# Attention visits of four scores instead of three where a visit holds an AV, from the fourth stage on

## The chip, the cores and the metric

The kernel runs on one core of a Trainium2 chip. The metric is the device time of one execution in microseconds (us). The engines that matter are TensorE (PE, matrix multiplies into PSUM), ScalarE (ACT), VectorE (DVE), GpSimd (POOL) and the queue of SyncE (SP), which issues most transfers. Each engine works through its own instructions in a fixed order, and waits on semaphores where it needs the result of another.

## The reference

Cosine attention over q, k, v of shape 8 x 12 x 448 x 64 (batch, heads, positions, width), then a feed-forward pair of matrices:

```
q_n = q / (norm(q) + 1e-6);  k_n = k / (norm(k) + 1e-6)
scores = q_n @ k_n.T / tau
attn = softmax(scores)
x = (attn @ v), heads side by side      # 3584 x 768
h = x @ w_in                            # 3584 x 2048
out = (h * cos(h)) @ w_out              # 3584 x 768
```

## The kernel before

**Units of work.** Two pairs of heads of one batch item make a quad; a batch item has three quads, the whole problem 24 (0 to 23). A quad is worked in seven steps. One step is a `scores` (L592 to L609): four 64 x 64 matmuls with 448 columns on PE (L601) into a pair of PSUM banks, then one exponential on ACT over 128 x 896 elements (L608), which empties that pair into a tile E. When all seven E of a quad exist, a `gather` (L628 to L649) does the quad's AV: 28 matmuls of E with V (L637) into a pair of banks, and a copy on DVE to AVs (L644). The row sums of two quads come from one `sums` (L711 to L755): 28 matmuls of E with a selecting matrix (L724) into one bank, Ln and Exp on ACT (L733, L734) for the reciprocal, a transfer by SP to a scratch tensor in memory (L737), four transfers by SP that read it back spread over the partitions (tile R, L743), and a product on POOL for each quad (L748), which writes xT, the input of the feed-forward part. Which quads share a round of sums is the list `ROUNDS` (L863); the last is quads 22 and 23.

**The feed-forward part.** m1 (L768 to L802) is, for one batch item, 96 matmuls of W1 with xT (L774) in eight pairs of banks; h * cos(h) of each pair runs through ACT (L792), DVE (L793), ACT (Sin, L795) and DVE (L798). Exponentials with Ln, and Sin, lie in two activation tables; a change of table is a load on ACT (L412). m2 (L823 to L857) multiplies the result with W2: sixteen matmuls of 384 columns (L833) for each half of an output tile of 128 rows, then a copy on DVE (L851) and, for each whole tile, transfers to the output by SP (L857).

**Stages.** The first three quads run in a head whose order is written out by hand. Then a loop over c = 0 to 7 (L1093 to L1194) makes eight stages. Stage c does m1 of batch item c, and after that m2 of the same item, into which the scores and AVs of later quads are woven: `STEPS` (L861) gives 35, 28, 21, 21, 21, 21, 0 and 0 steps, so quads 15 to 17 are scored in stage c = 3 (the fourth), 18 to 20 in c = 4, 21 to 23 in c = 5, and none in the last two.

**Visits.** Scores, AV and sums use tiles of 64 x 64 or 128 x 32 of the PE array, m1 and m2 the whole array. So the steps of a stage are cut into groups, called visits, by `visits_of` (L875 to L890). It takes `PER` = 3 steps for each. If a quad was finished in an earlier visit (`owed`), its AV is put into the visit behind two scores (`AT` = 2). A round of sums becomes due when its last quad is finished.

**Banks of a visit.** Scores and AVs take the three pairs of banks that m1 has left, in turn (`slot`, L892). So a score may start only when the exponential of the score (or the AV copy) three takings earlier has emptied its pair.

**Between visits** stands m2 work, cut to size by `fill(n)` (L1141): n matmuls of the list `items` of the stage. 24 come ahead of the first visit, 8 behind it (L1183, with nothing due), and behind every other visit a share of what is left: visits without an AV weigh 3, those with one 2 (`WE`), and `MOST` = 14 is the limit (L1182, L1183). `fill` also places a due round of sums, where the m2 tile that runs is between its fifth and its thirteenth matmul (L1138). In the last two stages, without visits, three banks serve m2, and a round that is still due goes in after ten matmuls (L1148 to L1150).

**Order on the engines.** The class `Planner` records each operation with a cost and what it reads and writes, and then orders ACT, DVE, POOL and SP by planned times. PE keeps the order of the program. Three short runs of operations are moved forward or back by their number (`LEADS`, L107 to L111); the run from operation 1169 lies in m1 of stage c = 4.

Of the kernel before, what the change touches and what calls it, by code (L numbers as in the profile page):

```python
# [304 lines left out]
def bass_cosine_attention__then__act_gcu_kernel(  # L305
# [16 lines left out]
    NNB = FF // 128  # L322
# [227 lines left out]
    def norm_b(qd, eng="pool", after=()):  # L550
        for _ in inverse(qd, 0, 2, after=after):
            pass
        for w in range(2):
            last = scale(qd, w, eng)
        return last
# [306 lines left out]
    MOST, WE = 14, (3, 2)  # L862
    ROUNDS = [[FIRST, FIRST + 1], [FIRST + 2]] + [[i, i + 1] for i in range(FIRST + 3, NQ, 2)]  # L863
    E1, E2, SLO, SHI = NNB - 6, NNB - 4, 4, 12
    PER, AT, EC = 3, 2, 0
    due = []
# [5 lines left out]

    owed, carried, events = [], [], [0]

    def visits_of(quads):  # L875

        steps = [divmod(g, NJ) for g in quads]
        out, late = [], []
        while steps:
            what, steps = steps[:PER], steps[PER:]  # L880
            mine, late = late, []
            for p, (qd, j) in enumerate(what):
                if j == NJ - 1:
                    (late if p or not steps else mine).extend(x for x in ROUNDS if x[-1] == qd)
            ended = [qd for qd, j in what if j == NJ - 1]
            if owed:
                what.insert(AT, (owed.pop(0), None))
            owed.extend(ended)
            out.append((what, mine))
        return out, late  # L890
# [5 lines left out]
    def visit(what):  # L896
        for qd, j in what:
            if j == 0:
                begin(qd)
            if j is None:  # L900
                gather(qd, slot())
            else:
                scores(NJ * qd + j, slot())
        for qd, j in what:
            if j == 0 and FIRST < qd < NQ - 3:
                norm_a(qd + 3, [o for o in P.ops if o.eng == "dve"][-1:])
            if j == 3 and FIRST < qd < NQ - 4:
                load_qk(qd + 4)
            if (qd, j) == (FIRST + 1, 3):
                bs = slot()  # L910
                for w in range(2):
                    transpose(FIRST + 2, w, bs + w)
            if j == NJ - 1 and qd + 2 < NQ:
                if qd > FIRST:
                    turn(qd + 2)
# [176 lines left out]
    done = NJ * FIRST  # L1092
    for c in range(B):  # L1093
# [47 lines left out]
        def fill(n):  # L1141
            while due and due[0][0] <= at[0] + n and len(banks) == 2 and at[0] + n < len(items) and not any(map(can_sum, range(at[0], at[0] + n))):
                n += 1
            n = min(n, len(items) - at[0])
            split = due and not can_sum(at[0])
            while n > 0:
                t, h, f0 = items[at[0]]
                if len(banks) == 3:  # L1148
                    if due and at[0] >= E1:
                        sums(due.pop(0)[1], free + 1)  # L1150
                elif due and can_sum(at[0]) and not (split and callable(due[0][1]) < can_sum(at[0] + n)):
                    what = due.pop(0)[1]
                    more = (what if callable(what) else lambda bk: sums(what, bk))(13 - cur[0])
                    due.extend((at[0] + 3 + 3 * i, x) for i, x in enumerate(more or ()))
                f1 = f0
                while n > 0 and f1 < NNB and items[at[0]:at[0] + 1] == [(t, h, f1)]:
                    at[0] += 1
                    f1 += 1
                    n -= 1
                    if due and can_sum(at[0]) and (n == 0 or not can_sum(at[0] + n)):  # L1160
                        break
                if (t, h) not in bank_of:
                    cur[0] = banks[(banks.index(cur[0]) + 1) % len(banks)] if cur[0] in banks else banks[0]
                    bank_of[t, h] = cur[0]
                m2(t, h, f0, f1, bank_of[t, h])
            if due and split and can_sum(at[0]) and not callable(due[0][1]) and len(banks) == 2:
                due.extend((at[0] + 3 + 3 * i, x) for i, x in enumerate(sums(due.pop(0)[1], 13 - cur[0]) or ()))

        new = done + STEPS[c]
        visits, over = visits_of(range(done, new))  # L1170
        if visits:
            visits[0][1].extend(carried)
            carried.clear()
            fill(FILLS[c][0] if c in FILLS else 2 * E2)
        for i, (what, mine) in enumerate(visits):
            if c == 0 and i == 1:
                spared.extend([x([o for o in P.ops if o.eng == "dve"][-1:]) for x in adds])
                norm_b(FIRST + 2, after=[o for o in P.ops if o.chain][-1:])
            visit(what)
            due.extend((0, r) for r in mine)  # L1180
            left = len(items) - at[0]
            weigh = [WE[sum(j is None for _, j in x)] for x, _ in visits[i:]]  # L1182
            even = 2 * (NNB - E2) + 3 * len(due) if i == 0 else min(MOST, -(-left * weigh[0] // sum(weigh)))  # L1183
            fill(FILLS[c][i + 1] if c in FILLS else even)
        if visits and new == NJ * NQ:
            gather(owed.pop(0), slot())
# [3 lines left out]
        done = new  # L1190
# [40 lines left out]
```

## Time and profile before

| what | value |
|---|---|
| median of three runs | 419.74 us (418.62 to 419.95) |
| the profiled execution | 419.27 us |
| its span in the trace | 417.5 us |
| PE busy | 408.4 us |
| ACT busy | 305.1 us |
| granted TensorE clock | 1.00 |

The span is the time from the first to the last recorded instruction; the execution has 1.77 us around it. Starts in the trace are counted from the start of the span. In the views, a line such as L601 is the line of the kernel that recorded the operation. A row of the timeline gives the start, the time, the engine, the line, what is written from what, and how many instructions are merged in it; a bracket behind it gives the idle time ahead of them and what ended it. A row of the chain of waits gives the start, the time and the engine whose work the end of the program hangs on there.

### The profile page before, as it was taken

What the parts mean: (1) busy time and instruction counts of PE and PEld (TensorE: products, weight loads), DVE (VectorE), ACT (ScalarE), POOL (GpSimd) and SP (SyncE); (2) the same over time, 40 slices, a digit from 0 to 9 for tenths busy, and PEclk for the clock granted to TensorE, in tenths of its full rate; (3) what the DMA queues carried; (4) which work ended last, traced back from release to release, by engine and by line L of the source; (5) the groups of instructions that cost most, each with busy time, mean ns of one, the idle gap of its engine ahead of it and who ended that gap; (6) DMA issues with size and microseconds to landing.
All of it is one profiled execution on the core that took longest, in us unless ns stands there. A gap on an engine that the chain in (4) does not pass through costs nothing.

```text
span 417.5 us, 8622 instructions
## 1 busy us (share of the span) xinstructions
PE 408.4 (98%) x3629; PEld 216.7 (52%) x3629; DVE 266.0 (64%) x359; ACT 305.1 (73%) x422; POOL 209.3 (50%) x145
## 2 busy tenths in 40 slices
PE   7999998999999999999999999999999999999997
PEld 7454544445554545555555555554554555555565
DVE  5887986638857549654985429845872328736931
ACT  6999899978888768897787747987797657605700
POOL 3668948996289862588419762477403113000000
PEclk9999999999999999999999999999999999999999
DMA  8999997999349994199617993099303523021023
GB/s 270 260 252 216 270 198 150 209 294 262 90 89 238 248 269 107 42 224 249 154 16 179 167 338 98 10 220 174 91 2 82 129 67 101 1 77 38 2 69 82
DMA packets 67223, 62.97 MB, mean 151 GB/s; under 512 B 36384, under 2 KB 59632, under 8 KB 67184
## 3 DMA queue, kind: packets, MB, share of 16 engines
q1 hardware_dynamic: 54816, 50.57, 47.9%
q0 software_dynamic: 12288, 11.80, 17.8%
q8 instruction: 28, 0.46, 0.4%
q14 instruction: 11, 0.09, 0.1%
q10 hardware_dynamic: 80, 0.05, 0.0%
HBM read 54.79 MB, written 11.15 MB: 158 GB/s over the span
## 4 chain that ended last, share of the span: by engine, by line
PE 80%; ACT 7%; DVE 5%; POOL 3%; DMA 2%; issue 1%; SPq 1%; POOLq 0%
PE PS L833 32%; PE PS L774 31%; PE PS L601 7%; PE PS L637 6%; ACT E L608 4%; PE PS L724 3%; DVE gT L798 2%; DVE ar L793 1%; DMA Qf<-in_q_dram 1%; DMA Kf<-in_k_dram 1%; POOL Qn L542 1%; POOL sqq L491 1%; PE PS L810 1%; ACT ar L676 1%; DVE AVs L644 1%
## 5 line engine op out<-in xcount | busy, mean ns | idle before, releaser
L608 ACT ACTIVATE E<-PS 128x896 bf16<-128x896 f32 x168 | 143.5, 921 | 20.5 <-PE PS L601 19.2
L833 PE MATMUL PS<-W,gT 128*128 128x384 bf16 x880 | 153.4, 327 | 0.0
L774 PE MATMUL PS<-xT,W 128*128 128x448 bf16 x768 | 147.7, 353 | 0.4 <-POOL xT L748 0.3
L833 PEld LDWEIGHTS PS<-W,gT 128*128 128x128 bf16 x880 | 81.9, 98 | 69.1 <-issue 16.0
L774 PEld LDWEIGHTS PS<-xT,W 128*128 128x128 bf16 x768 | 74.3, 98 | 71.3 <-issue 1.5
L792 ACT ACTIVATE ar<-PS 128x896 int32<-128x896 f32 (+1 forms) x72 | 58.8, 827 | 47.0 <-PE PS L774 46.9
L793 DVE SCALAR_TENSOR_TENSOR ar<-ar,PS 128x896 f32<-128x896 int32 (+1 forms) x72 | 69.2, 980 | 34.0 <-ACT ar L792 34.0
L748 POOL TENSOR_TENSOR xT<-AVs,R 128x896 bf16<-128x896 f32 x20 | 41.7, 2089 | 65.9 <-DMA R<-rscr 65.9
L798 DVE TENSOR_TENSOR gT<-PS,ar 128x896 bf16<-128x896 f32 (+1 forms) x72 | 69.3, 983 | 1.9 <-ACT ar L795 1.6
L795 ACT ACTIVATE ar<-ar 128x896 f32<-128x896 f32 (+1 forms) x72 | 60.6, 861 | 8.5 <-DVE ar L793 7.8
L851 DVE COPY osb<-PS 128x384 f32<-128x384 f32 x54 | 30.0, 556 | 53.6 <-PE PS L833 52.9
L542 POOL TENSOR_TENSOR Qn<-Qf,rr 128x896 bf16<-128x896 f32 x21 | 35.4, 1685 | 44.5 <-DVE rr L530 44.4
L601 PE MATMUL PS<-qT,kT 64*64 64x448 bf16 x672 | 48.9, 358 | 2.8 <-DVE kT L575 1.4
L644 DVE COPY AVs<-PS 128x896 f32<-128x896 f32 x21 | 22.8, 1088 | 35.3 <-PE PS L637 35.3
L491 POOL TENSOR_TENSOR sqq<-Qf 128x896 bf16<-128x896 f32 x21 | 35.2, 1677 | 7.3 <-DVE n L495 5.5
L491 POOL TENSOR_TENSOR sqk<-Kf 128x896 bf16<-128x896 f32 x21 | 35.2, 1676 | 6.2 <-DVE Kn L542 6.1
L542 POOL TENSOR_TENSOR Kn<-Kf,rr 128x896 bf16<-128x896 f32 (+1 forms) x22 | 36.7, 1666 | 0.0
L637 PE MATMUL PS<-E,Vb 64*64 64x448 bf16 x588 | 31.5, 350 | 0.4 <-ACT E L608 0.4
L601 PEld LDWEIGHTS PS<-qT,kT 64*64 64x64 bf16 x672 | 15.2, 105 | 27.3 <-issue 10.9
L451 POOL DMA_DIRECT2D Vb<-in_v_dram x24 | 18.1, 755 | 16.7 <-PE PS L601 10.3
L495 DVE TENSOR_REDUCE n<-sqk 128x14 f32<-128x896 bf16 (+2 forms) x24 | 24.9, 1039 | 1.8 <-POOL sqk L491 1.2
L495 DVE TENSOR_REDUCE n<-sqq 128x14 f32<-128x896 bf16 (+2 forms) x24 | 24.8, 1037 | 0.8 <-POOL sqq L491 0.6
(68 smaller groups left out, 200.5 us busy)
## 6 DMA issues: line engine op xcount, KB each, us to landing
Qf<-in_q_dram SPq DMA_DIRECT2D x24, 448.0 KB, 5.1
out_dram<-osb SPq DMA_DIRECT2D x54, 192.0 KB, 2.8
Kf<-in_k_dram SPq DMA_DIRECT2D x23, 448.0 KB, 6.1
R<-rscr SPq DMA_DIRECT2D x40, 224.0 KB, 4.4
Vb<-in_v_dram POOLq DMA_DIRECT2D x24, 224.0 KB, 5.9
W<-in_moe_w_in_dram POOLq DMA_DIRECT2D x4, 768.0 KB, 10.7
W<-in_moe_w_out_dram POOLq DMA_DIRECT2D x4, 768.0 KB, 12.5
Kf<-in_k_dram SPq DMA_DIRECT2D x1, 320.0 KB, 4.6
```

The source lines that it names most:

```text
L491: op(eng, (1.64 if eng == "pool" else 1.05) * n, lambda e: e.tensor_tensor(dst, src, src, ALU.mult), r=cut(nm + "f", s, part), w=at, after ...
L495: return op("dve", 0.05 + 0.94 * n, lambda e: e.tensor_reduce(out=n2[u].ap()[:, H * w:H * w + H] if part == ALL[0] else jr(n2[u], w, part) ...
L542: lambda e: e.tensor_tensor(n[u].ap()[:, j0:j1].rearrange("p j r d -> p r j d"), f[s].ap()[:, :, j0:j1], rb, ALU.mult),
L601: ins = e.matmul(bank(bs + r, S, 64 * a, 64 * a + 64), kT[u].ap()[64 * r:64 * r + 64, j, a, :], qT[u].ap()[64 * r:64 * r + 64, :, a, :], s ...
L608: act("exp", 0.806, lambda e: e.activation(E[es].ap(), two(bs), ACT.Exp, bias=0.0, scale=INV_TAU), r=pair(bs), w=[("E", es)], chain="E")
L637: ins = e.matmul(bank(bs + a, S, 64 * r, 64 * r + 64), Vb[vs].ap()[64 * a:64 * a + 64, r, j, :], E[es[j]].ap()[64 * a:64 * a + 64, r, :], ...
L774: ins = e.matmul(bank(bk + i2), W1.ap()[:, i, 128 * nb:128 * nb + 128], xT[c % 2].ap()[:, i, :], start=(i == 0), stop=(i == NKC - 1))
L792: op("act", 0.055 + 0.375 * n, lambda e: e.activation(ai, src, ACT.Identity, bias=0.25, scale=INV2PI), r=bs, w=at)
L793: op("dve", 0.06 + 0.47 * n, lambda e: e.scalar_tensor_tensor(a, ai, -2.0 * math.pi, src, ALU.mult, ALU.add), r=bs + at, w=at)
L795: act("sin", 0.09 + 0.375 * n, lambda e: e.activation(a, a, ACT.Sin, bias=GUARD * math.pi / 2.0, scale=GUARD), r=at, w=at)
L798: op("dve", 0.07 + 0.47 * n, lambda e: e.tensor_tensor(gT.ap()[:, f0:f1, col:col + S], src, a, ALU.mult), r=bs + at, w=[("g", c % 2, f) fo ...
L833: ins = e.matmul(bank(bk, HW), gT.ap()[:, f, col:col + 128], W2.ap()[:, f, HW * h:HW * h + HW], start=(f == 0), stop=(f == NNB - 1))
```

## The change

`visits_of` gets the number of the stage. From c = 3 on, a visit into which an AV falls takes four steps instead of three; the others still take three. The AV keeps its place behind two scores, so that two scores follow it. From c = 3 on all visits have the same weight, and the limit of a share is 20 instead of 14.

```
-    def visits_of(quads):
+    def visits_of(quads, c):
...
-            what, steps = steps[:PER], steps[PER:]
+            per = 4 if owed and c >= 3 else PER
+            what, steps = steps[:per], steps[per:]
...
-        visits, over = visits_of(range(done, new))
+        visits, over = visits_of(range(done, new), c)
...
-            weigh = [WE[sum(j is None for _, j in x)] for x, _ in visits[i:]]
-            even = 2 * (NNB - E2) + 3 * len(due) if i == 0 else min(MOST, -(-left * weigh[0] // sum(weigh)))
+            weigh = [3 if c >= 3 else WE[sum(j is None for _, j in x)] for x, _ in visits[i:]]
+            even = 2 * (NNB - E2) + 3 * len(due) if i == 0 else min(20 if c >= 3 else MOST, -(-left * weigh[0] // sum(weigh)))
```

In the built program, PE's order from stage c = 3 on reads as follows (numbers of matmuls; "sc" scores, four to a step):

| stage | before | after |
|---|---|---|
| c = 3 | sc 8, AV, sc 4, m2 8; sc 12, m2 14; sc 12, m2 14, sums; sc 8, AV, sc 4, m2 14; sc 12, m2 14; sc 8, AV, sc 4, m2 14; sc 12, m2 26 | sc 8, AV, sc 8, m2 8; sc 12, m2 20; sc 8, AV, sc 8, sums, m2 19; sc 12, m2 19; sc 8, AV, sc 8, m2 19; sc 12, m2 19 |
| c = 4 | seven visits, m2 8, 12, 12, 8, 12, sums and 8, 12 behind them | six visits, m2 8, 13, 13, 13, sums and 13, 12 |
| c = 5 | seven visits, m2 8, 14, 14 and sums, 14, 14, 14, 14; AV of quad 23, sums of 22 and 23, m2 12 | six visits, m2 8, 20, sums and 19, 19, 19, 19; AV of quad 23 |
| c = 6 | m1, m2 96 | m1, m2 10, sums of 22 and 23, m2 86 |

The operations of stage c = 4 have numbers lower by two, so the run of `LEADS` from 1169 falls on operations two later in the same chain.

## Prediction

> **What bounds the kernel now.** I read the page first: busy times, granted clock, the chain that ended last.
>
> ```profile
> span 417.5 us, 8622 instructions
> ...
> PE 408.4 (98%) x3629; PEld 216.7 (52%) x3629; DVE 266.0 (64%) x359; ACT 305.1 (73%) x422; POOL 209.3 (50%) x145
> ...
> PE 80%; ACT 7%; DVE 5%; POOL 3%; DMA 2%; issue 1%; SPq 1%; POOLq 0%
> ```
>
> The end hangs on PE for 80% of the span. An average over stages isn't enough, so I asked for the stretches between m1 and m1 of c = 3, 4 and 5, the only ones that the change cuts anew.
>
> ```profile
> 210.40:245.90 35.50, 35.50 (x366) 18.59 (x364) 19.19 (x30) 24.47 (x35) 24.74 (x17) 1.00 0.73 157
> 261.90:288.60 26.70, 26.70 (x295) 13.66 (x292) 16.51 (x25) 23.53 (x34) 19.57 (x14) 1.00 0.66 131
> 306.70:341.50 34.80, 34.80 (x382) 18.20 (x380) 12.18 (x19) 24.79 (x33) 7.45 (x4) 1.00 0.31 75
> ```
>
> The columns are stretch, length, and busy time of PE, weight load, DVE, ACT and POOL, then the granted clock. PE is busy for the whole of each stretch at clock 1.00, and ACT comes next (23.53 of 26.70 us at c = 4). So whatever PE is spared or made to wait there moves the end one for one. Then the chain of waits, to see what PE's time consists of.
>
> ```profile
> 218.42 2.38 PE PS L833 x14
> 221.50 2.38 PE PS L833 x14
> 223.88 1.44 PE PS L724 x28
> 225.82 1.32 PE PS L637 x28
> ...
> 393.51 18.20 PE PS L833 x112
> ```
>
> 112 matmuls of m2 in one run take 18.20 us, 0.1625 each. The AV's 28 take 1.32, or 0.19 for four, which is also the price of a score.
>
> **What a visit costs.** Between 218.42 and 221.50 lie 14 matmuls of m2 and three scores: 3.08 us. The matmuls are 14 x 0.1625 = 2.275 and the scores 3 x 0.19 = 0.57. The remaining 0.235 is the price of going over to the small tiles and back. In PE's order a stage of 21 scores is now cut into six visits (4, 3, 4, 3, 4, 3) instead of seven; the number of AVs, scores, sums and m2 matmuls is the same. Three stages lose one visit each: **3 x 0.235 = -0.7 us**.
>
> **What a fourth score costs.** An AV visit now takes five pairs of banks from a ring of three: the first score pair a, the second b, the AV c, the third score a, the fourth b. So the fourth may start only when ACT has read the second score out of b. Before, only the third score came back to a used pair. The AV visit that opens c = 5 in the timeline:
>
> ```profile
> 310.56 0.57 PE L601 MATMUL PS<-qT,kT 64*64 64x448 bf16 x8
> 310.96 1.49 PE L637 MATMUL PS<-E,Vb 64*64 64x448 bf16 x28
> 311.00 1.73 ACT L608 ACTIVATE E<-PS 128x896 bf16<-128x896 f32 x2 [0.15 <-PE PS L601]
> 312.29 0.36 PE L601 MATMUL PS<-qT,kT 64*64 64x448 bf16 x4
> ```
>
> The first two exponentials begin 0.44 us behind the first score and together last 1.73, until 312.73. The third score starts at 312.29; the fourth could follow at 312.29 + 0.19 = 312.48, but b isn't free. How soon PE goes on after an exponential that it waits for is seen in the head, where it waited:
>
> ```profile
> 20.00 0.92 ACT L608 ACTIVATE E<-PS 128x896 bf16<-128x896 f32 x1
> ...
> 20.97 0.38 PE L601 MATMUL PS<-qT,kT 64*64 64x448 bf16 x4 [0.43 <-ACT E L608]
> ```
>
> The exponential ends at 20.92 and PE starts at 20.97, 0.05 later. So the fourth score starts at 312.73 + 0.05 = 312.78: PE waits 0.30 us. Behind the waiting score stand the m2 matmuls of the visit (and the sums, once in each stage), and everything after them. ACT cannot make up for it, as PE is the bound. There are nine such visits: **9 x 0.30 = +2.7 us**, the term that decides.
>
> Its bounds: where Ln of a sums stands ahead of the exponentials, they come later.
>
> ```profile
> 225.25 0.57 PE L601 MATMUL PS<-qT,kT 64*64 64x448 bf16 x8
> 225.37 0.54 ACT L733 ACTIVATE Zs<-PS 128x448 f32<-128x448 f32 x1 [1.29 <-PE PS L724]
> 225.81 1.72 ACT L608 ACTIVATE E<-PS 128x896 bf16<-128x896 f32 x2
> 226.97 0.36 PE L601 MATMUL PS<-qT,kT 64*64 64x448 bf16 x4
> ```
>
> Here b is free at 227.53 + 0.05 = 227.58, against 226.97 + 0.19 = 227.16: a wait of 0.42, 3.8 us for nine. After the change the sums stand behind the four scores, so I don't take that value. At the other end, exponentials in a row begin 0.81 us apart (1.73 - 0.92). Were b given free when the next exponential begins, and not when the recorded one ends, each wait would be 0.11 shorter: 0.19, or 1.7 us. The row at 20.97 speaks for the recorded end; I take 0.30.
>
> **The late sums.** At c = 5 the new shares use up all m2 matmuls ahead of the AV of quad 23, so the sums of quads 22 and 23 move from there to c = 6, behind ten m2 matmuls. They come between two pieces of m2 instead of between an AV and m2, one change of tiles more: 2.38 - 2.275 = 0.105, **+0.1 us**. More matters what hangs on them: xT of quads 22 and 23, which m1 of c = 7 reads. Before, there were 18 us of m1 and 16 of m2 to cover the chain; now only the m2.
>
> ```profile
> 337.96 1.51 PE L724 MATMUL PS<-E,sel 128*32 128x448 bf16 x28
> ...
> 339.51 0.54 ACT L733 ACTIVATE Zs<-PS 128x448 f32<-128x448 f32 x1 [3.11 <-PE PS L724]
> 340.09 0.58 ACT L734 ACTIVATE Zs<-Zs 128x448 f32<-128x448 f32 x1
> 340.69 1.28 ACT L412 ACT_TABLE_LOAD   x1
> 340.69 0.58 SPq L737 DMA_DIRECT2D rscr<-Zs  x1
> ...
> 343.35 2.46 SPq L743 DMA_DIRECT2D R<-rscr  x4
> ...
> 347.95 4.15 POOL L748 TENSOR_TENSOR xT<-AVs,R 128x896 bf16<-128x896 f32 x2 [11.89 <-DMA R<-rscr]
> ...
> 359.52 15.76 PE L833 MATMUL PS<-W,gT 128*128 128x384 bf16 x96
> ...
> 360.35 1.88 ACT L795 ACTIVATE ar<-ar 128x896 f32<-128x896 f32 x3
> ```
>
> Set at the old m2 start, 359.52: ten matmuls (1.63) and a change of tiles bring the sums to 361.25, and to 362.7 they run. ACT is done with Sin at 362.23, loads the exponential's table (1.28) and starts Ln at 363.55. Ln takes 0.58, Exp 0.60 until SP issues: 364.73. From that issue to the first read back are 2.66 us (343.35 - 340.69), from there to the first product 4.60, and two products take 4.15: 367.4, 372.0, 376.1. m1 of c = 7 comes after 96 m2 matmuls and the sums, 359.52 + 15.6 + 1.54 = 376.7. It reads quad 22 (done at 374.1) 0.4 us later, quad 23 only after eight matmuls, at 378.2. About **2 us of cover** are left, so the cost is nothing. The second table load, back to Sin, and the queue of output transfers behind the read-back on SP hide under the same m2 work: ACT's next Sin comes with m1 of c = 7, and there are three output buffers.
>
> The Trainium skill, "ScalarE: Activation LUTs", section "What ACT_TABLE_LOAD costs", gives a switch of tables 1.28 us of load and 1.38 of drain. This trace shows the 1.28 and no drain: Exp ends at 340.67 and the load starts at 340.69. By the page one drain would fall into the chain and leave 0.6 us of cover, which hides it still.
>
> **What else moves, at nothing.** At c = 4 POOL does the product of quad 17 and a V load ahead of the scaling of Q and K for quad 20.
>
> ```profile
> 265.74 0.57 PE L601 MATMUL PS<-qT,kT 64*64 64x448 bf16 x8
> ...
> 268.56 1.69 POOL L542 TENSOR_TENSOR Kn<-Kf,rr 128x896 bf16<-128x896 f32 x1
> 270.20 2.09 POOL L748 TENSOR_TENSOR xT<-AVs,R 128x896 bf16<-128x896 f32 x1
> ...
> 273.65 1.29 SPq L585 DMA_TRANSPOSE kT<-Kn  x1
> ...
> 275.51 0.76 POOL L451 DMA_DIRECT2D Vb<-in_v_dram  x1
> ...
> DMA to landing us min/median/max: 3.0/3.0/3.7
> ```
>
> The scaling of K, now over at 270.25, then ends 2.09 + 0.76 later, near 273.1, and its transposition is issued by 275.2 and lands by 278.9. Quad 20 is first scored in the fifth visit. Its start: 265.74 for the first, + 3.9 (scores with the wait 2.5, m2 1.4), + 2.9 (three scores, 13 m2), + 4.7, + 2.9, or 280.1. Cover 1.2 us; gone, each us costs one. The longer shares of m2 (19 and 20) leave ACT idle and free the banks sooner, nothing for PE. The shifted `LEADS` give m1 of c = 4 the order on ACT that c = 3 has; m1 there takes as long for each matmul (18.16 for 96 against 15.99 for 84), so nothing.
>
> ```profile
> 192.25 18.16 PE PS L774 x96
> ...
> 245.91 15.99 PE PS L774 x84
> ```
>
> **Sum.** -0.7 + 2.7 + 0.1 = +2.1 us. The profiled execution took 419.27 (its span of 417.5 and 1.77 around it): 421.4. The median of the runs shown lies 0.47 higher, 419.74, so I give **421.8 us**.
>
> **Rivals.** (1) *The fourth score doesn't wait.* If ACT frees b in time, only the visits saved are left: -0.7 + 0.1 = -0.6, 419.1 us. The point is a wait of 0.6 / 9 = 0.07 us a visit: b would have to be free 0.23 us earlier than in the rows. For it: ACT is idle ahead of each visit. Against: in both visits shown the second exponential ends 0.2 to 0.4 us after the fourth score could start, and nothing in the change makes the first start sooner. 8%. (2) *The last round comes late.* If scratch write, read-back or products take over 2 us longer than the rows (they share the queue with output transfers), m1 of c = 7 waits: for 1 to 2 us beyond the cover 422.8 to 423.8. Against: in that stretch SP has little else, and POOL nothing. 9%. (3) *The clock falls.* Nine new waits are small gaps in which PE idles at a change of banks; if the granted clock fell to half for them, over only the 26.7 us of c = 4, that adds 26.7 us: 446 us. Against it stands the head of this kernel, where PE idled 1.9 of 24 us, the same waits among them, at clock 1.00:
>
> ```profile
> 10.00:34.00 24.00, 22.11 (x364) 11.81 (x365) 20.34 (x30) 23.65 (x35) 15.05 (x14) 1.00 1.11 251
> ```
>
> 1%. (The Trainium skill, "TensorE: Matmul & The Clock Gate", section "A second HAM failure mode: psum-queue depth-cycling", tells of a kernel whose clock swings to half speed for such gaps. In this trace the head doesn't bear it out.) That the program doesn't do what it says is ruled out by its order on PE.
>
> **How the numbers follow.** The forecast, nine waits of 0.19 to 0.42, gets 80%: with the other terms +1.1 to +3.2, or 420.8 to 422.9; 2% are left for what I don't see (the transposition's cover among it). The three runs shown lie 1.3 us apart, so I widen both ends a little: **420.4 to 423.2**. Left out are rival 1, rival 3 and part of rival 2. A difference of 0.3%, 1.26 us, is about what a measurement of this kernel can tell from no change. Slower by more than that: the forecast but for its lowest end (69%), rivals 2 and 3 (10%): 79%. Within: that lowest end (11%), most of rival 1 (6%) and half of the rest: 18%. Faster: rival 1 with the scatter, and the other half: 3%.
>
> **What would show it.** In each of the nine AV visits the last four scoring matmuls start about 0.5 us after the four before them instead of 0.2, put down to ACT L608; m1 starts 0.7 us later than before at c = 4 and 1.3 at c = 5. No idle time of PE ahead of L774 in c = 7, and a product of POOL ending near its start. It is wrong if the last four follow at 0.2, or if PE stands ahead of m1 of c = 7.

## The result and the profile after

The changed kernel takes 421.02 us (median of seven runs, 420.56 to 422.9); the kernel before, run beside it, 418.78 (seven, 418.45 to 419.95). The ratio is 1.0053 with a 95% interval of 1.004 to 1.0066: **slower by 2.2 us** (0.5%), where +2.1 was forecast. The time forecast, 421.8, lies 0.8 above the measured one: it was counted from the 419.74 of three runs of the kernel before, and the seven runs give 418.78.

The page of the changed kernel, its first lines:

```profile
span 419.1 us, 8621 instructions
...
PE 408.6 (98%) x3629; PEld 216.2 (52%) x3629; DVE 266.3 (64%) x359; ACT 308.5 (74%) x424; POOL 209.4 (50%) x145
```

PE has as many instructions as before and nearly the same busy time (408.4 there). On this page the change can't be seen, but for ACT's two instructions more, two table loads (L412) of 1.28 us around the late sums. The three stretches, each from the first m2 matmul to the start of the next m1 (columns: stretch, length, busy time of PE, weight load, DVE, ACT and POOL, granted clock, DMA share and GB/s). The first one is cut shorter than the view of the kernel before, which went on to 245.90 and took in 12 matmuls of m1 and 28 of sums:

```profile
209.76:242.29 32.53, 32.15 (x326) 17.05 (x324) 18.42 (x28) 23.99 (x34) 23.21 (x16) 1.00 0.72 156
262.00:289.32 27.32, 26.94 (x293) 13.93 (x292) 17.02 (x26) 23.52 (x34) 20.35 (x14) 1.00 0.61 120
307.48:341.46 33.98, 33.60 (x354) 17.65 (x352) 11.99 (x19) 24.35 (x31) 7.46 (x4) 1.00 0.31 77
```

PE was busy for the whole of each; now 0.38 are missing in each, with the clock still at 1.00. The recorded ends of matmuls are modelled, so this is less than what is lost. Where the time goes is seen in the chain of waits. First the kernel before, its first AV visit of c = 3 and the m2 work ahead and behind:

```profile
210.41 3.90 PE PS L833 x24
214.31 0.50 PE PS L601 x8
214.81 1.32 PE PS L637 x28
216.14 0.19 PE PS L601 x4
216.32 1.41 PE PS L833 x8
```

The same place in the changed kernel:

```profile
209.76 3.90 PE PS L833 x24
213.66 0.34 PE PS L601 x4
214.00 0.02 issue
214.03 1.73 ACT E L608 x2
215.76 0.04 issue
215.81 0.38 PE PS L601 x4
216.19 1.41 PE PS L833 x8
```

Before, the end hung on PE alone: two scores, the AV, one score, 2.01 us from 214.31 to 216.32. Now it hangs on the first score, then on two exponentials of ACT, and then on the fourth score: 2.53 us from 213.66 to 216.19. The score that was added is 0.19 of the 0.52; the other 0.33 is new waiting. The timeline of the changed kernel shows the wait itself, in the row of the weight load (PEld):

```profile
214.03 3.43 ACT L608 ACTIVATE E<-PS 128x896 bf16<-128x896 f32 x4
...
215.32 0.87 PE L601 MATMUL PS<-qT,kT 64*64 64x448 bf16 x8
...
215.80 0.11 PEld L601 LDWEIGHTS PS<-qT,kT 64*64 64x64 bf16 x4 [0.55 <-ACT E L608]
```

The third score starts at 215.32, the fourth at 215.81 (chain), 0.49 later. The row of PE merges both into one stretch of 0.87 and shows no gap; whoever asks the waits of PE from 209 to 415 gets an empty list. The waits of the weight load in the same window have them (us in total, times, longest), first the changed kernel, then the kernel before:

```profile
PEld PS L601 <- ACT E L608: 5.0, 9, 0.6
...
PEld PS L601 <- ACT E L608: 1.3, 4, 0.3
```

Nine times, as there are nine AV visits, and each up to 0.6; the four of the kernel before are shorter, and none of them stands on its chain. (The weight load runs ahead: for the third score it starts at 215.13, 0.19 before the matmuls. So its 0.55 is longer than what PE loses, 0.30.) The chain of the last stages, with the late sums:

```profile
359.73 1.63 PE PS L833 x10
361.35 1.44 PE PS L724 x28
362.79 14.08 PE PS L833 x86
376.87 18.23 PE PS L774 x96
...
413.30 2.65 PE PS L810 x32
```

The sums stand between two pieces of m2, as said, and m1 of c = 7 follows at 376.87 with no wait ahead of it.

**A sharper measure.** Executions of one kernel differ by 1 to 4 us (29 of the kernel before lie between 418.26 and 422.57). Much of that arises ahead of c = 3: the first m2 matmul of c = 3 starts anywhere from 209.4 to 213.2 us in the fourteen traces. What the change does lies between that start (210.41 before, 209.76 after) and the start of the last matmuls, L810 (411.71 before, 413.30 after). That stretch took 201.30 us before and 203.54 after: **+2.24**, as the medians say. Every experiment below is read by it too, from one trace each. By their times alone e1, e3, e4, e5, e6 and e12 can't be told from the kernel before, as their intervals reach 1:

| kernel | ratio to before, 95% interval | stretch, from its two rows | against before |
|---|---|---|---|
| after | 1.0053 (1.004 to 1.0066) | 209.76 to 413.30 | +2.24 |
| e1, shares alone | 1.0008 (0.998 to 1.0036) | 210.00 to 411.74 | +0.44 |
| e2, four scores alone | 1.011 (1.0068 to 1.0152) | 210.82 to 417.35 | +5.23 |
| e3, after with half exponentials | 0.9977 (0.9949 to 1.0006) | 211.20 to 411.85 | -0.65 |
| e4, before with half exponentials | 1.0001 (0.9971 to 1.003) | 213.20 to 414.51 | +0.01 |
| e5, c = 4 alone | 1.0022 (1.0 to 1.0044) | 210.41 to 412.38 | +0.67 |
| e6, late sums alone | 1.0006 (0.9994 to 1.0019) | 209.94 to 411.35 | +0.11 |
| e7, after with padded AVs | 1.0098 (1.0079 to 1.0117) | 209.38 to 415.70 | +5.02 |
| e8, before with padded AVs | 1.0128 (1.0108 to 1.0147) | 210.05 to 417.03 | +5.68 |
| e9, e2 without a lead | 1.0064 (1.004 to 1.0088) | 209.60 to 413.63 | +2.73 |
| e10, after with the lead moved | 1.005 (1.0028 to 1.0073) | 210.85 to 414.39 | +2.24 |
| e11, sums still later | 1.0095 (1.0073 to 1.0118) | 210.66 to 416.69 | +4.73 |
| e12, before without the lead | 1.0012 (0.9993 to 1.003) | 209.62 to 410.93 | +0.01 |

In two of them, e4 and e12, PE's work and waits should be those of before, and they are within 0.01 us of it; e10 should equal the changed kernel, and does. So fine did this stretch measure in these three pairs.

### The profile page after: what moved, and what is told of

Read it like the earlier page. It is cut to its first block, busy times and chain, and to the rows that moved or that the text cites. A ratio compares the mean times of both kernels' runs of the same rounds, so it can differ in the third digit from the quotient of the medians.

```text
span 419.1 us, 8621 instructions
## 1 busy us (share of the span) xinstructions
PE 408.6 (98%) x3629; PEld 216.2 (52%) x3629; DVE 266.3 (64%) x359; ACT 308.5 (74%) x424; POOL 209.4 (50%) x145
## 4 chain that ended last, share of the span: by engine, by line
PE 82%; ACT 11%; DVE 5%; DMA 1%; issue 0%; SPq 0%
PE PS L833 34%; PE PS L774 31%; ACT E L608 8%; PE PS L601 7%; PE PS L637 4%; PE PS L724 4%; DVE gT L798 2%; DVE ar L793 1%; DMA Kf<-in_k_dram 1%; PE PS L810 1%; ACT ar L676 1%; DVE n L495 0%; PE PS L759 0%; ACT ar L792 0%; ACT ar L682 0%
## 5 line engine op out<-in xcount | busy, mean ns | idle before, releaser
L608 ACT ACTIVATE E<-PS 128x896 bf16<-128x896 f32 x168 | 143.4, 920 | 26.8 <-PE PS L601 24.9
L601 PE MATMUL PS<-qT,kT 64*64 64x448 bf16 x672 | 50.1, 359 | 3.9 <-DVE kT L575 1.4
L451 POOL DMA_DIRECT2D Vb<-in_v_dram x24 | 18.2, 758 | 26.8 <-PE PS L601 20.7
```

What stands on the lines that cost most here:

```text
L601: ins = e.matmul(bank(bs + r, S, 64 * a, 64 * a + 64), kT[u].ap()[64 * r:64 * r + 64, j, a, :], qT[u].ap()[64 * r:64 * r + 64, :, a, :], s ...
L608: act("exp", 0.806, lambda e: e.activation(E[es].ap(), two(bs), ACT.Exp, bias=0.0, scale=INV_TAU), r=pair(bs), w=[("E", es)], chain="E")
```

## The experiments

The theory (W): the fourth score waits about 0.3 us for the second exponential, nine times; three visits saved give 0.235 each. The rival (S): the cost comes from the shares and from what the new order brings late, and the four scores themselves only save visits.

**e1 and e2: the two halves of the change.** e1 is the kernel before with the equal weights and the limit of 20; e2 has the visits of four with the old shares.

```
e1:
-            weigh = [WE[sum(j is None for _, j in x)] for x, _ in visits[i:]]
+            weigh = [3 if c >= 3 else WE[sum(j is None for _, j in x)] for x, _ in visits[i:]]
-            even = ... else min(MOST, ...)
+            even = ... else min(20 if c >= 3 else MOST, ...)
e2:
+            per = 4 if owed and c >= 3 else PER
+            what, steps = steps[:per], steps[per:]
```

> Three scores in every visit as before, and only the even shares of m2 with the limit of 20. The theory (W) is that the fourth score waits for the second exponential, 0.30 us in each of nine visits, and that this is the cost: none of those waits is here, seven visits a stage stay, and only the sums come between two pieces of m2 three times, 0.1 us each. W expects +0.3 us against the kernel before (about 0.1%). The rival (S) is that the cost lies in the moved shares of m2 and the moved sums: S expects all of it, +2.2 us (0.5%).

> Four scores in a visit with an AV from the fourth stage on, but the shares of m2 by the old weights and the old limit of 14, and so the last sums in their old place. W: nine waits of 0.30 us less three visits of 0.235 us, +2.0 us against before (0.5%). S: the shares are the old ones, so only the visits saved are left, -0.7 us (-0.2%).

e1 gave +0.44: not the shares, as W says. Three rounds of sums come to lie between two pieces of m2 there, each with one change of tiles more, and 3 x 0.105 is 0.32, as expected. The other 0.12 lies in two visits of c = 4: in the chain of e1 twelve score matmuls take 0.75 at 271.51 instead of 0.69, and an AV 1.38 at 281.15 instead of 1.32. e2 gave +5.23, which neither expected. By stages: c = 4 and c = 5 cost +0.67 and +0.73, as in W, but the stretch from c = 3 to the m2 of c = 4 costs 3.83. Its chain of waits there:

```profile
243.63 2.08 POOL xT L748
...
245.76 0.93 PE PS L774 x4
...
261.65 2.01 DVE gT L798 x2
...
263.71 2.44 PE PS L774 x12
```

PE waits twice in m1 of c = 4: for x of quad 14 (0.9 us by the waits of PE) and for g (1.9). Behind each wait PE loses 0.16 more (the last twelve matmuls take 2.44 us, twelve in a row 2.27). With the 0.73 of a stage that makes the 3.8.

Why x comes late is read from the first m2 matmul of c = 3 on (210.82 in e2, 209.76 in the changed kernel). With the old shares the sums of quads 14 and 15 start 15.74 us behind it, with the even shares 14.34. The scratch write comes 21.68 behind it instead of 17.08, as in e2 the second step of the reciprocal stands behind three exponentials of scores. The first product comes 32.81 behind it instead of 24.88, with the read-back behind output transfers on SP. So the even shares are a condition of the change; how much of the delay each of these steps makes was not tried one by one.

**e9, e10 and e12: the lead.** The second wait of e2 is at the place that the entry 1169 of `LEADS` orders. e9 is e2 without it, e12 the kernel before without it, and e10 the changed kernel with 1167, the number that the operations now have.

```
     LEADS = (
-        (1169, 8, -11.0),
```

> The run with four scores and the old shares (+4.6 us against before instead of the +2.0 expected), now without the entry of LEADS that begins at operation 1169. In that run's trace PE waits twice ahead of m1 of c = 4: 0.9 us for xT of quad 14, whose sums come 2.5 us later there, and 1.9 us for gT of an earlier pair. Theory: the second wait is the entry of LEADS, which falls on other operations as the numbers have shifted by one; without it ACT and DVE keep the plain order, so the 1.9 us go: +2.7 us against before. Rival: it follows from the late sums, like the first, and stays: +4.6 us.

> The changed kernel with that entry of LEADS set back by two, to 1167, so that it falls on the same operations as in the kernel before. The prediction took the shift to cost nothing: the same time as the changed kernel, +2.2 us against before. Rival: part of the cost is the shift, then less.

> The control for the runs on LEADS: the kernel before without the entry from operation 1169. m1 of c = 4 takes as long for each matmul as m1 of c = 3, which has no such entry, so 0 us against before.

e9 gave +2.73: the wait for g is gone, and of the waits of PE this is left (its lines are one lower):

```profile
PE PS L773 <- POOL xT L747: 0.4, 1, 0.4
```

e9 is 2.50 below e2. The wait for g makes 1.9 of it, with 0.16 behind it; the rest is x, which came 0.5 earlier in e9, and one trace each doesn't show that this is the entry's doing. In the changed kernel the entry's place does nothing (e10: +2.24, as after), and in the kernel before the entry itself does nothing in this stretch (e12: +0.01). The order on DVE shows what differs in e2. First e2, then the same place of the changed kernel:

```profile
261.57 3.08 DVE L798 TENSOR_TENSOR gT<-PS,ar 128x896 bf16<-128x896 f32 x3
...
259.45 2.19 DVE L798 TENSOR_TENSOR gT<-PS,ar 128x896 bf16<-128x896 f32 x2
```

Three products of full width that write g stand in a row in e2, and PE (263.71) and ACT (263.69) wait for the third. The changed kernel, e1, e9 and e12 have one and the same order in this m1, and e10 has that of the kernel before; none of them has three such products in a row. The late x is no longer felt by then: up to the product at 257.03 all of DVE's work in this m1 starts 2.21 us later than in the kernel before, as PE's sums do. This speaks for the order, which the entry sets by number, and not for the late x as the cause of the second wait. Whether it is only that the numbers in e2 are shifted was not tried with a corrected number there.

**e3 and e4: take the wait away by faster exponentials.** From quad 15 on the exponential is cut to half its width. So b is free sooner, and PE's work is unchanged; half of each E is then not computed. e3 has this in the changed kernel, e4 in the one before.

```
-        act("exp", 0.806, lambda e: e.activation(E[es].ap(), two(bs), ...
+        w = S // 2 if qd >= 15 else S
+        act("exp", 0.806, lambda e: e.activation(E[es].ap()[:, :, 0:w], two(bs)[:, :, 0:w], ...
```

> The changed kernel, but from quad 15 on (fourth stage) the exponential of a score covers only half its columns; the other half of E keeps old values. The order of all engines stays. Each exponential then takes about 0.5 us instead of 0.9, so the second ends before PE gets to the fourth score. W: the waits are gone and the visits saved remain, -0.6 us against before (-0.15%). S and any rival that doesn't put the cost into the exponentials: +2.2 us as the change itself.

> The control for the run with half exponentials: the kernel before, from quad 15 on with half the columns in each exponential (the other half of E keeps old values). In the kernel before PE waits for no exponential in these stages, so W expects 0.0 us against before. If ScalarE's own load were the bound there (a rival, A), some us less.

e3 gave -0.65 and e4 +0.01. The first AV visit of c = 3 in the chain of e3 (its lines are one higher):

```profile
215.10 0.50 PE PS L601 x8
215.60 1.32 PE PS L638 x28
216.92 0.38 PE PS L601 x8
217.30 1.41 PE PS L834 x8
```

ACT is off the chain, and the visit takes 2.20, which is the 2.01 of three scores and 0.19 for the fourth. With the waits gone, what is left of the change is the gain of three visits: -0.65, where -0.705 + 0.105 makes -0.60. The waits are therefore 2.24 + 0.65 = 2.89 us, or **0.32 for each of nine**. It is a diagnosis, not a version to keep.

**e5 and e6: one part alone.** e5 makes the whole change in c = 4 only; e6 moves only the last sums of the kernel before into c = 6.

```
e5:
+            per = 4 if owed and c == 4 else PER
+            weigh = [3 if c == 4 else WE[...] ...]
+            even = ... else min(20 if c == 4 else MOST, ...)
e6:
+        held = due[:] if visits and new == NJ * NQ else []
+        if held:
+            due.clear()
...
+        due.extend(held)
```

> The change in the fifth stage (c = 4) alone: six visits there, the old visits and shares in the others, the last sums in their old place. W: three waits of 0.30 us less one visit of 0.235 us, +0.67 us against before (0.16%), a third of the whole. A rival (L) that puts the cost into the sums of quads 22 and 23, which move to c = 6 in the change: 0 us or -0.2.

> The kernel before, with only the last round of sums moved from the end of c = 5 to c = 6, behind ten m2 matmuls, as the change has it. W: one change of tiles more, +0.1 us against before, with idle cover left ahead of m1 of c = 7. L: most of the cost, +1.5 to 2.2 us.

Both came out as expected: +0.67 for three waits and a visit saved (3 x 0.32 - 0.235 = 0.73, less 0.06 that the eight m2 matmuls behind the sums of c = 4 took longer before: 1.47 at 284.35, and 1.41 elsewhere), and +0.11 for the late sums.

**e7 and e8: give PE something to do meanwhile.** Six matmuls with zero weights stand behind the AV, adding nothing to its banks, in the changed kernel (e7) and in the one before (e8). What PE would have waited, the pad fills for nothing in e7; in e8 it costs its whole time.

```
+            for r in range(6 if qd >= 14 else 0):
+                ins = e.matmul(bank(bs + 1, S, 64 * (r % 2), 64 * (r % 2) + 64), zeros[64:128, 0:64],
+                               E[es[0]].ap()[64:128, r % 2, :], start=False, stop=(r >= 4))
```

> The changed kernel with six matmuls of zeros more at the end of each AV from quad 14 on (ten AVs; they add zero to one bank, so nothing changes in the output). Four matmuls take 0.19 us, so six are 0.28 us of PE work. W: in nine visits the fourth score waits 0.30 us anyway, the six matmuls lie inside that wait and cost nothing; only at the AV of quad 23, with no score behind it, they cost 0.28. So +2.24 + 0.3 = +2.5 us against the kernel before. If PE isn't idle there (against W): +2.24 + 2.8 = +5.0 us.

> The same six matmuls of zeros at the end of each AV from quad 14 on, in the kernel before, where no score waits. W: all ten cost their 0.28 us, +2.8 us against before (0.7%).

Both sizes were missed: +5.02 and +5.68. By its size alone e7 met the value named against W, +5.0. But a pad of six takes 0.57 us, not 0.28, so neither value applies as it stands. An AV visit in the chain of e8 (L642 is the pad, and lines behind it are three higher):

```profile
327.08 0.18 PE PS L601 x2
327.26 0.39 PE PS L642 x6
327.65 0.19 PE PS L601 x2
327.84 2.38 PE PS L836 x14
```

From the AV's end at 327.08 to m2 it takes 0.76 instead of 0.19. And one of e7, with four scores:

```profile
320.70 0.50 PE PS L601 x8
...
322.53 0.18 PE PS L601 x2
322.71 0.39 PE PS L642 x6
323.10 0.38 PE PS L601 x6
323.48 1.44 PE PS L727 x28
```

The rows still answer the question. No exponential stands on the chain of e7, and its visit of 2.78 (320.70 to 323.48) is 2.01 + 0.19 + 0.57 with no wait. Without pads a visit of the changed kernel takes 2.53. The same pad costs 0.57 in three-score visits and 0.25 in four-score visits; the missing **0.32 were waiting time**. In the whole stretch: 5.68 with pads over before, 5.02 - 2.24 = 2.78 over the changed kernel, a difference of 2.90 = 9 x 0.32. Two ways of removing the wait (e3, and this) agree on its size.

**e11: how much cover the late sums have.** As e6, but the sums of quads 22 and 23 go in behind 48 matmuls of m2 instead of ten, 38 x 0.1625 = 6.2 us later.

```
-                    if due and at[0] >= E1:
+                    if due and at[0] >= 48:
```

> The kernel before with the last round of sums in c = 6 not behind 10 but behind 48 matmuls of m2, 38 x 0.1625 = 6.2 us later than in the run with late sums. The trace of the changed kernel shows 2.9 us of cover between the last product on POOL and its first use in m1 of c = 7, and 0.7 us in which the sums wait for the end of Sin on ACT, which isn't so here. Theory: m1 of c = 7 waits 6.2 - 2.9 - 0.7 = 2.6 us, +2.7 us against before with the change of tiles. If the chain had much more cover than read, 0.

It gave +4.73, 4.62 more than e6. A wait came, near the expected 2.6, in the chain of waits:

```profile
366.30 1.44 PE PS L724 x28
...
376.34 2.08 POOL xT L748
...
378.47 20.02 PE PS L774 x96
```

PE waits 2.8 us for x of quad 22. It is made up otherwise than expected, which was reckoned with quad 23: the read-back is issued 2.6 us behind the scratch write (368.97, 371.58) instead of the 1.73 of the changed kernel, behind an output transfer at 371.07 on the same queue. And m1 then takes 20.02 us where it takes 18.2 in the kernel before and in the changed one. The reason stands in the stretches of e11 (columns as above; the granted clock is third from the end):

```profile
375.60:378.40 2.80, 0.05 (x1) 0.00 (x0) 0.56 (x1) 0.00 (x0) 2.06 (x1) 1.00 0.96 250
378.40:382.20 3.80, 3.73 (x11) 1.51 (x12) 0.00 (x0) 0.00 (x0) 2.09 (x2) 0.55 0.18 52
382.20:398.00 15.80, 15.80 (x85) 8.17 (x84) 12.48 (x12) 11.64 (x14) 0.00 (x0) 1.00 0.00 0
```

Behind the idle 2.8 us the clock is at 0.55 for 3.8 us, and m1 loses 1.8: 2.8 + 1.8 + 0.1 = 4.7. The cover is finite: past it, this run paid for the wait and for the clock.

## Why the prediction was right, point by point

- **PE is the bound, every us there moves the end.** Right. The chain is PE from c = 3 to the end but for the nine waits, and the stretch's +2.24 is the whole difference of the medians.
- **Three visits saved, 3 x 0.235.** Right: with the waits gone, -0.65 is left (e3).
- **The fourth score waits 0.30 for the second exponential.** Right in mechanism and place; e3 and e7 each take it away alone. The size is 0.32: 0.30 until the start, as worked out from 312.73 + 0.05, and 0.02 behind it (from the last score to m2 the timeline has 0.31 us, 215.81 to 216.12, and before 0.29, 215.97 to 216.26). The fourth score starts 0.05 behind the recorded end of the exponential (215.76, then 215.81), as in the head. Neither bound, 0.19 or 0.42, was met, and the Ln ahead of exponentials that would have given 0.42 now stands behind them.
- **The late sums, +0.1 and 2 us of cover.** The price is right (e6, +0.11). The cover was understated. In the timeline of the changed kernel:

```profile
362.30 1.28 ACT L412 ACT_TABLE_LOAD   x1
363.61 0.54 ACT L733 ACTIVATE Zs<-PS 128x448 f32<-128x448 f32 x1
...
364.79 0.58 SPq L737 DMA_DIRECT2D rscr<-Zs  x1
366.52 2.40 SPq L743 DMA_DIRECT2D R<-rscr  x4
371.31 4.11 POOL L748 TENSOR_TENSOR xT<-AVs,R 128x896 bf16<-128x896 f32 x2 [35.40 <-DMA R<-rscr]
```

  Sums, Ln and scratch write come within 0.1 us of the forecast. From the write to the read-back are 1.73 us instead of the 2.66 taken from the row of before, so the products end at 375.42 instead of 376.1. Quad 23 is needed behind eight matmuls of m1, at 376.87 + 1.5 = 378.4: about 2.9 us of cover. The step cost nothing either way. Of the drain that the Trainium skill names for a switch of tables ("ScalarE: Activation LUTs", section "What ACT_TABLE_LOAD costs") there is again nothing to see: Sin ends 0.02 ahead of the load (362.28), and Ln starts 0.03 behind the end of it.
- **Transposition, lead and longer shares at nothing.** Right, for the changed kernel: no wait on kT, 18.2 us for each m1, and e10 for the lead. The order on DVE and ACT in this m1 is indeed the plain one, as without the entry. The transposition was issued by 275.58 and lands 2.9 us later, 278.5, for a score at 280.32, so its cover was 1.8, not 1.2. But "nothing" hung on the even shares, which the prediction didn't say: without them x of quad 14 comes late (0.9 us of wait in e2, 0.4 in e9). And the entry of `LEADS`, harmless here as argued, costs a wait of 1.9 in e2, where its operations come in another order.
- **Rival 1 (no wait)** is what e3 makes of the kernel, and it gave the time worked out for it, -0.65 against -0.6. **Rival 2 (the last round late)** didn't come, with about 2.9 us of cover; e11 shows it does come when the sums start 6.2 us later, and part of it is the queue shared with output transfers that the rival named. Its price there was larger than the wait, since the clock fell. **Rival 3 (the clock)** didn't come: nine gaps of 0.3 us, clock 0.999 to 1.00 in all seven runs.
- **What would show it.** The fourth score 0.49 behind the third, named; put down to ACT L608, nine times. From the m2 of c = 3, m1 of c = 4 starts 0.73 later and m1 of c = 5 1.40 later (named: 0.7 and 1.3).

That three terms gave +2.1 and +2.24 was measured is not luck in the sum. The wait from the pads (9 x 0.32), the visits at the forecast's price (-0.705) and the late sums from e6 (+0.11) make +2.28, less the 0.06 at c = 4. No two large errors cancel: the largest miss of a term is the wait, 2.9 against 2.7.

## What to carry to other kernels

Count the takings of a ring of buffers in each group of work before you make the group larger: a step that comes back to a used slot waits if the slot's reader isn't done. The third score came back to one in both kernels without a wait, the fourth with one. What the larger group saves in changes of tiles (0.235 here, three times) must pay for that wait (0.32, nine times). An engine that is 74% busy can still stand on the critical path if it is asked for two things in a row and the bound engine waits at that moment. And an order that is written by position or by share holds only as long as the operations keep their numbers and times: change the one and look at what the other covered.

## What the runs showed of the hardware that wasn't expected

- **The pad's matmuls took twice as long each.** AV, scores and sums use 64 x 64 or 128 x 32 tiles in all four places, and 28 matmuls of an AV take 1.32 us, 0.047 each. The pad's six matmuls all read rows 64 to 127, in two column halves, so that only two of the four 64 x 64 tiles are used: 0.57 us, 0.095 each. That the unused half is the reason fits the factor of two; it was not tried by itself, and the pad differs in another way too: all six write one bank.
- **The clock fell behind an idle stretch of 2.8 us, and not behind one of 1.9.** In e11 PE idles from 375.65 to 378.47 and the clock is then 0.50 for about 3.4 us (0.66 in 378.6 to 379.2, 0.50 until 382.1, 0.83 in 382.1 to 382.4); the mean clock is 0.996 in all four runs of e11. In e2 PE waits 1.9 us in one piece, and the stretch behind it has 1.00 in the trace. These are two places in two traces and no measured limit; 3 of 74 runs of the kernel before, and one of the six of e2, have a mean clock of 0.995 or 0.996 too, for a reason that no trace shows. The Trainium skill, "TensorE: Matmul & The Clock Gate", section "What's actually happening", tells of a window of about 3.4 us; the length of the slow time agrees with it, but the idle stretch was shorter than that.
- **A gap of 0.3 us is not listed among the waits of PE.** The nine gaps cost 2.9 us, 0.7% of the time, and show only in the chain of waits and in the weight load's waits.
